# Hash bits of three heads: one test over 128 partitions and copies within SBUF, in place of four tests of six partitions

## The chip, the core and the metric

The kernel runs on one core of a Trainium2 chip. A core has five engines that work side by side, each through its own queue of instructions in order: TensorE (PE, matrix products, with PEld for its weight loads), VectorE (DVE), ScalarE (ACT), GpSimd (POOL) and SyncE (SP, which issues transfers). SBUF is the working memory of 128 partitions, PSUM the smaller one into which TensorE writes; GpSimd does not read PSUM here. The metric is the time of one execution on the device in microseconds (us). All times below that are not durations count from the start of the profiled span.

## The reference

Attention within hash buckets, and then a feed-forward layer with a maximum of three products. Shapes: batch 4, 8 heads, 768 positions, head width 64, 6 hash bits; the second part has 3072 tokens, width 512, inner width 768.

```python
q_bits = (np.einsum('bhsd,dk->bhsk', q, proj) > 0)     # k_bits in the same way
q_bucket = np.sum(q_bits * powers, axis=-1)
mask = q_bucket[:, :, :, None] == k_bucket[:, :, None, :]
scores = np.where(mask, scale * q @ k.T, -1e9)
attn = softmax(scores) @ v
h = np.maximum(np.maximum(x @ w1, x @ w2), x @ w3)     # x: attn with the heads side by side
out = h @ w_out
```

## The kernel before

**The mask as part of the product.** A tile S holds, for one head, the 64 rows of the transposed q (or k) in partitions 0 to 63 and the hash bits, as +0.5 or -0.5, in the partitions from 64 on. One product of 70 rows then gives the score plus the number of bits that agree, and the exponential of ScalarE (L292) subtracts the full number, so that pairs of other buckets come out at nearly zero. So before the scores of a head can be computed, its q and k must be transposed and scaled (the "placement") and its bits tested and put under them.

**Batch 0 in pairs of heads.** The first batch comes in four pairs of heads. For each pair, side (1 is k, 0 is q) and head, the steps are: three transposes by TensorE into a PSUM tile mp (pair_turn, L132); a copy of mp into an SBUF tile T32 by VectorE or ScalarE (pair_keep, L138); a scaled copy into S by GpSimd (pair_place, L143); the hash product of T32 with the projection (TensorE, into a PSUM tile bp); and the test of the hash against zero, which gives the bits. The positions of a head are held in two halves ("par" 0 and 1 of 384 each), one in partitions 0 to 63 of T32 and one in 64 to 127.

For pair 0 and pair 1 the hash is made head by head: first_hash (L171) multiplies with two six-column pieces of the projection, so that for side and par the six bits lie in partitions 32j to 32j+5 of bp, j = 2 side + par. first_bits (L177) tests one such piece: VectorE reads six partitions of bp from PSUM and writes 6x384 bits to their place in S. A head takes four of these. For pairs 2 and 3, pair_hash (L149) fills 128 partitions, tests them in one operation into a tile "bits", and four transfers by SP carry them into S.

**The order of the work** is written out by hand. The scores are cut into units u = 0, 1, 2, ... of two key blocks each: scores(u) issues two products (L290) into an sc tile and one exponential. Twelve units cover a pair in batch 0: units 0 to 5 are head 0 of pair 0, 6 to 11 head 1, 12 to 23 pair 1. `when(u, f)` hangs other work on unit u, in the order of its registration. For pair 1 the transposes and copies stand on units 1, 1, 2 and 4, the hashes (head_hash) on 3 and 6, the bits (head_bits) on the same units and the ones after. The tuple `cs` says for each of the four copies, in the order key and query of head 0, key and query of head 1, whether ScalarE (1) or VectorE (0) makes it. The copies of pair 2 stand on units 5, 6, 9 and 10; the second is the key copy of head 1.

Two rings of PSUM tiles matter. Up to unit 10, mp and bp tiles take the tags m0 to m3 in turn, so that a tile waits until the one four places earlier has been read. From unit 11 on there is a third sc buffer, laid over two of these tags, so unit 11 waits until the tiles in them have been read, and mp and bp share the two that are left.

**Projection tiles.** pst is the projection as loaded. GpSimd copies it into pj2 (L470, 128x32, the two halves of the projection interleaved for the two pars) and into pj (L472, for the later batches' quads of heads), before its first placement.

The call of the bits in the first head's second half and in pair 1:

```python
for side, par in ((1, 0), (0, 0), (1, 1)):
    first_bits(bp, side, 1, par)          # pair 0, head 1; the fourth on unit 1
...
def head_bits(pi, hd, n):
    side, par = ((1, 0), (0, 0), (1, 1), (0, 1))[n]
    first_bits(parts[pi, hd], side, hd, par, pi)
```

Of the kernel before, what the change touches and what calls it, by code (L numbers as in the profile page):

```python
# [9 lines left out]
FP32 = mybir.dt.float32  # L10
FP16 = mybir.dt.float16
BF16 = mybir.dt.bfloat16
AluOp = mybir.AluOpType
# [4 lines left out]
def kernel(  # L18
# [12 lines left out]
    nc = tc.nc  # L31
    B, H, S, D = q.shape
    NBITS = proj.shape[1]
    P = 128
    NM = S // P
    HALF = S // 2
# [5 lines left out]
    Q = 32  # L42
# [15 lines left out]
    konst = ctx.enter_context(tc.tile_pool(name="konst", bufs=1))  # L58
# [1 line left out]
    t32_pool = ctx.enter_context(tc.tile_pool(name="t32", bufs=3))  # L60
    t16_pool = ctx.enter_context(tc.tile_pool(name="t16", bufs=2))
    s_pool = ctx.enter_context(tc.tile_pool(name="spool", bufs=6))
    b_pool = ctx.enter_context(tc.tile_pool(name="bpool", bufs=2))
    vo_pool = ctx.enter_context(tc.tile_pool(name="vopool", bufs=4))
    small = ctx.enter_context(tc.tile_pool(name="small", bufs=4))
    ys_pool = ctx.enter_context(tc.tile_pool(name="yspool", bufs=1))
# [11 lines left out]
    def lay_out(**tags):  # L78
        rings.update(tags)
        if "pool" in rings:  # L80
            third.close()
        rings["pool"] = third.enter_context(tc.tile_pool(name="third_ps", bufs=1, space=bass.MemoryType.PSUM))
# [3 lines left out]
    def ps_tile(name, kind="ms"):  # L86
        if kind == "ms" and spare:
            return spare.pop(0)
        tag = rings[kind].pop(0)
        rings[kind].append(tag)  # L90
        shape = [P, 2, 512] if kind == "sc" else [P, 512]
        return (rings["pool"] if tag in ("s2", "m2", "m3") else fixed_ps).tile(shape, FP32, tag=tag, name=name)
# [2 lines left out]
    iden = konst.tile([P, P], FP32, name="iden")  # L95
    pj = konst.tile([P, 2, Q], FP32, name="pj")
    pj2 = konst.tile([P, Q], FP32, name="pj2")
    pst = konst.tile([Q, 2, NBITS], FP32, name="pst")
    ones = konst.tile([P, 3, Q], FP16, name="ones")
    warm = konst.tile([P, HALF], FP16, name="warm")  # L100
# [7 lines left out]
    nat, t32, t16, s_of, where, v_at = {}, {}, {}, {}, {}, {}  # L108
# [6 lines left out]
    def s_tile(name):  # L115
        if name not in s_of:
            s_of[name] = s_pool.tile([D + KB, 4, S], BF16, tag="S", name="S")
        return s_of[name]


    def load_pair(pi, eng, sides=(1, 0), h0=0, h1=2):
        if pi not in nat:
            start_set(pi, [(0, 2 * pi), (0, 2 * pi + 1), (1, 2 * pi), (1, 2 * pi + 1)])
        n = nat[pi].rearrange("p (s h w) -> p s h w", s=2, h=2)
        for side in sides:
            src = (q, k)[side][0, 2 * pi + h0 : 2 * pi + h1].rearrange("h (p c) d -> p h (c d)", p=P)
            eng.dma_start(n[:, side, h0:h1, :], src)
# [12 lines left out]
    def pair_place(pi, side, par, h0=0, h1=2):  # L140
        o = s_tile(pi)[0:D, 2 * side + h0 : 2 * side + h1, par * HALF : (par + 1) * HALF]
        i_ = t32[pi][par * D : (par + 1) * D, side, h0 * HALF : h1 * HALF].rearrange("d (h n) -> d h n", n=HALF)
        nc.gpsimd.tensor_scalar(out=o, in0=i_, scalar1=RS, scalar2=1.0, op0=AluOp.mult, op1=AluOp.mult)  # L143
# [27 lines left out]
    def first_hash(bp, side, hd, pi=0):  # L171
        for par in range(2):
            j = 2 * side + par
            nc.tensor.matmul(bp[Q * j : Q * j + NBITS, 0:HALF], pj2[:, par : 2 * NBITS : 2],  # L174
                             t32[pi][:, side, hd * HALF : (hd + 1) * HALF], start=True, stop=True)

    def first_bits(bp, side, hd, par, pi=0):  # L177
        j = 2 * side + par
        nc.vector.tensor_scalar(out=s_of[pi][D : D + NBITS, 2 * side + hd, par * HALF : (par + 1) * HALF],  # L179
                                in0=bp[Q * j : Q * j + NBITS, 0:HALF], scalar1=0.0, scalar2=0.5,  # L180
                                op0=AluOp.is_gt, op1=AluOp.subtract)


    def load_quad(side, g, xs, eng):
# [263 lines left out]
    def when(u, f, *args):  # L448
        at.setdefault(u, []).append(lambda: f(*args))

    with tc.manual_schedule():
# [7 lines left out]
        load_pair(1, nc.sync)  # L459
        load_pair(2, nc.sync)  # L460
        nc.gpsimd.memset(pj[:], 0.0)
        nc.vector.memset(pj2[:], 0.0)
        nc.vector.memset(ones[:], 1.0)
        nc.vector.memset(ones[:, 1, Q // 2 :], 0.0)
        nc.vector.memset(ones[:, 2, : Q // 2], 0.0)
        for t in at_tiles:
            nc.vector.memset(t[:, :, HALF : HALF + 2], 1.0)
        for hd in range(2):
            for u in range(2):
                nc.gpsimd.tensor_copy(pj2[hd * D + u * Q : hd * D + (u + 1) * Q, hd : hd + 2 * NBITS - 1 : 2], pst[:, u, :])  # L470
        for x in range(4):
            nc.gpsimd.tensor_copy(pj[x * Q : (x + 1) * Q, :, x : x + 4 * NBITS - 3 : 4], pst[:])  # L472
        lay_out(sc=["s0", "s1"], ms=["m0", "m1", "m2", "m3"])
        wp = ps_tile("wp", "sc")[:, 0, :]
        mq, mk, bk, bq = ps_tile("mp"), ps_tile("mp"), ps_tile("bp"), ps_tile("bp")
# [4 lines left out]
        pair_keep(0, 1, 0, mk)  # L480
        pair_keep(0, 0, 0, mq, nc.scalar.copy)
        first_hash(bk, 1, 0)
        first_hash(bq, 0, 0)
        mk1 = ps_tile("mp")
        pair_turn(0, 1, 1, mk1)
        for side, par, mp, bp in ((1, 0, mk, bk), (0, 0, mq, bq), (1, 1, mk, bk)):
            first_place(side, 0, par, mp)
            first_bits(bp, side, 0, par)
        pair_place(0, 0, 1, 0, 1)
        pair_keep(0, 1, 1, mk1, nc.scalar.copy)  # L490
        first_bits(bq, 0, 0, 1)
        mq1 = ps_tile("mp")
        pair_turn(0, 0, 1, mq1)
        pair_keep(0, 0, 1, mq1, nc.scalar.copy)
        scores(0)
        rest = []

        def first_rest():
            bp = ps_tile("bp")
            rest.append(bp)  # L500
            for side in (1, 0):
                first_hash(bp, side, 1)
                for par in range(2):
                    pair_place(0, side, par, 1, 2)
            for side, par in ((1, 0), (0, 0), (1, 1)):
                first_bits(bp, side, 1, par)
            t32.pop(0)

        when(0, first_rest)
        when(1, lambda: first_bits(rest[0], 0, 1, 1))  # L510

        def head_hash(pi, hd, last):
            bp = parts[pi, hd] = ps_tile("bp")
# [4 lines left out]

        def head_bits(pi, hd, n):
            side, par = ((1, 0), (0, 0), (1, 1), (0, 1))[n]  # L520
            first_bits(parts[pi, hd], side, hd, par, pi)

        parts = {}
        for pi, us, hs, offs, by_head, cs in ((1, (1, 1, 2, 4), (3, 6), (0, 0, 1, 1), 0, (1, 1, 0, 1)),):
            for u, c, (side, hd) in zip(us, cs, ((1, 0), (0, 0), (1, 1), (0, 1))):
                when(u, pair_group, pi, side, hd, nc.scalar.copy if c else nc.vector.tensor_copy)
                if hd == 1 or by_head:
                    for par in range(2):
                        when(u, pair_place, pi, side, par, *((hd, hd + 1) if by_head else ()))
            for hd in range(2):  # L530
                when(hs[hd], head_hash, pi, hd, hd == 1)
                for n in range(4):
                    when(hs[hd] + offs[n], head_bits, pi, hd, n)
# [16 lines left out]
        for g in range(2, NPAIR // 2):  # L550
# [3 lines left out]
            for n, side in enumerate((1, 0)):  # L554
                name = (side, g)
# [122 lines left out]
```

## Time and profile before

| what | us |
|---|---|
| median of 3 runs (260.29 to 260.9) | 260.55 |
| profiled execution, its own time | 260.33 |
| its span, first to last instruction | 258.6 |
| TensorE busy | 252.3 |
| VectorE busy | 207.9 |
| ScalarE busy | 182.0 |
| GpSimd busy | 77.7 |
| L179 (bits of six partitions), 16 times | 8.9 |
| L138 on VectorE, 8 times | 4.5 |
| L143 (placements), 17 times | 12.4 |

The time of the profiled execution is 1.7 us more than the span of its instructions. The busy time of TensorE contains matmuls that overlap in its pipeline. Rows of a timeline give start, duration, engine (a q behind it: its queue), line, operation, tile written and tiles read, shapes, and how often; in brackets stands idle time of the engine before it and what ended it. Tile names lose their numbers: T is T32, pj stands for pj and pj2.

### The profile page before, as it was taken

Reading aid. Unit: us, or ns where it says so; the run is one execution under the profiler, and the core shown is the slowest. Engines: PE = TensorE matmul, PEld = TensorE weight load, DVE = VectorE, ACT = ScalarE, POOL = GpSimd, SP = SyncE. Lnnn points to the kernel's source line nnn. Section 1 sums busy time; section 2 is a strip of 40 time slices with the busy share of each in tenths; the row PEclk is TensorE's granted clock in tenths of the full one; section 3 lists DMA queues with packets and bytes.
Section 4 is the critical chain, followed back from the end, with each engine's and each line's share of the span. In section 5 each row is a group of like instructions: output and inputs, shape, how many; then the busy total and the mean of one; then the engine's idle time right before and its main releaser. Section 6 shows DMA issues by size and latency. Waiting matters only on the chain.

```text
span 258.6 us, 5894 instructions
## 1 busy us (share of the span) xinstructions
PE 252.3 (98%) x2207; PEld 139.0 (54%) x2207; DVE 207.9 (80%) x474; ACT 182.0 (70%) x276; POOL 77.7 (30%) x128
## 2 busy tenths in 40 slices
PE   7999999999999999999999999999999999999994
PEld 3454444555555555555555555555555555555552
DVE  2794989999989997999989998998758984884450
ACT  3999887939994589909995589909995689612322
POOL 3599921694617119221416116100000000000000
PEclk9999999999999999999999999999999999999998
DMA  7998997659983707670283806320120003001203
GB/s 213 379 243 123 188 267 194 190 135 204 168 252 83 178 3 163 202 193 11 57 248 68 193 3 135 109 71 11 42 81 3 0 3 122 3 0 38 87 0 122
DMA packets 22251, 30.92 MB, mean 120 GB/s; under 512 B 3056, under 2 KB 17744, under 8 KB 22224
## 3 DMA queue, kind: packets, MB, share of 16 engines
q0 software_dynamic: 9088, 12.59, 25.6%
q1 hardware_dynamic: 12848, 17.58, 21.2%
q8 instruction: 17, 0.28, 0.5%
q10 hardware_dynamic: 288, 0.39, 0.5%
q14 instruction: 10, 0.08, 0.1%
HBM read 25.17 MB, written 6.29 MB: 122 GB/s over the span
## 4 chain that ended last, share of the span: by engine, by line
PE 91%; DVE 6%; issue 1%; ACT 0%; DVEq 0%
PE l L405 36%; PE sc L290 23%; PE l L436 12%; PE av L317 10%; PE bp L218 3%; PE mp L132 2%; DVE xT L386 2%; DVE T L197 1%; PE bp L174 1%; PE sm L367 1%; PE wp L477 1%; DVE S L179 1%; PE bp L154 1%; DVE rb L374 1%; PE l L425 1%
## 5 line engine op out<-in xcount | busy, mean ns | idle before, releaser
L292 ACT ACTIVATE AT<-sc 128x768 f16<-128x768 f32 x192 | 152.6, 823 | 45.9 <-PE sc L290 39.2
L405 PE MATMUL l<-xT,w_sb 128*128 128x384 f16 x568 | 112.1, 325 | 0.0
L290 PE MATMUL sc<-S 72*128 72x384 bf16 (+1 forms) x384 | 91.7, 326 | 0.7 <-ACT AT L292 0.6
L405 PEld LDWEIGHTS <-w_sb 128*128 128x128 f16 x576 | 55.4, 97 | 39.2 <-DVE xT L386 1.2
L414 DVE TENSOR_TENSOR ht<-ht,l 128x384 f16<-128x384 f16 x95 | 52.2, 550 | 20.6 <-PE l L405 17.9
L290 PEld LDWEIGHTS <-S 72*128 72x128 bf16 (+1 forms) x384 | 36.1, 98 | 33.9 <-issue 8.3
L202 POOL TENSOR_SCALAR T<-T 128x768 bf16<-128x768 f32 x24 | 22.4, 934 | 79.1 <-DVE T L197 42.8
L436 PE MATMUL l<-wout_sb,ht 128*128 128x512 f16 x138 | 36.0, 378 | 0.0
L342 DVE TENSOR_TENSOR As<-As,AT 128x768 f16<-128x768 f16 x52 | 33.9, 653 | 2.1
L317 PE MATMUL av<-AT,vo 128*32 128x385 f16 x744 | 34.2, 327 | 0.2 <-DVE xT L386 0.2
L342 DVE TENSOR_TENSOR As<-AT,AT 128x768 f16<-128x768 f16 x52 | 29.6, 568 | 4.6 <-ACT AT L292 4.6
L412 ACT CAST ht<-l 128x384 f16<-128x384 f32 x47 | 22.5, 478 | 10.4 <-DVE ht L414 5.9
L317 PEld LDWEIGHTS <-vo 128*32 128x32 f16 x768 | 19.5, 96 | 15.3 <-issue 6.4
L197 DVE STREAM_TRANSPOSE T<-nat 128x384 f32<-128x384 f32 x48 | 26.5, 564 | 0.2 <-DMA S<-bits 0.2
L386 DVE SCALAR_TENSOR_TENSOR xT<-av,sv,rb 128x384 f16<-128x384 f32 (+1 forms) x35 | 21.6, 618 | 1.2
L436 PEld LDWEIGHTS <-ht 128*128 128x128 f16 x138 | 13.3, 97 | 12.5
L344 DVE TENSOR_TENSOR As<-As 128x384 f16<-128x384 f16 x48 | 17.2, 358 | 1.7
L440 ACT COPY osb<-l 128x512 f32<-128x512 f32 x23 | 13.4, 582 | 6.5 <-PE l L436 6.5
L248 POOL DMA_DIRECT2D vo<-in_v_dram x24 | 13.3, 570 | 2.8 <-DMA wout_sb<-in_moe_w_out_dram 1.6
L143 POOL TENSOR_SCALAR S<-T 64x768 bf16<-64x768 f32 (+1 forms) x17 | 12.4, 731 | 3.7 <-DVE T L138 1.8
L179 DVE TENSOR_SCALAR S<-bp 6x384 bf16<-6x384 f32 x16 | 8.9, 554 | 2.4 <-PE bp L174 2.1
L374 DVE STREAM_TRANSPOSE rb<-rr 128x384 f32<-128x384 f32 x16 | 9.1, 566 | 0.1
(55 smaller groups left out, 115.8 us busy)
## 6 DMA issues: line engine op xcount, KB each, us to landing
out_dram<-osb SPq DMA_DIRECT2D x23, 256.0 KB
S<-T SPq DMA_DIRECT2D x48, 96.0 KB
nat<-in_k_dram POOLq DMA_DIRECT2D x16, 192.0 KB, 4.7
nat<-in_q_dram POOLq DMA_DIRECT2D x16, 192.0 KB, 5.7
w_sb<-in_moe_w_dram POOLq DMA_DIRECT2D x12, 192.0 KB, 4.6
vo<-in_v_dram POOLq DMA_DIRECT2D x24, 96.0 KB, 5.3
nat<-in_k_dram SPq DMA_DIRECT2D x10, 192.0 KB
nat<-in_q_dram SPq DMA_DIRECT2D x8, 192.0 KB
```

The lines of the kernel that those rows point to most:

```text
L197: nc.vector.transpose(t32[name][:, u, half * HALF : (half + 1) * HALF], i_)
L202: nc.gpsimd.tensor_scalar(out=t16[name][:, u, :], in0=t32[name][:, u, :], scalar1=RS, scalar2=1.0, op0=AluOp.mult, op1=AluOp.mult)
L290: nc.tensor.matmul(sc[:, j, 0:HALF], s_of[kn][0 : D + nb, kx, m * P : (m + 1) * P], s_of[qn][0 : D + nb, qx, qh * HALF : (qh + 1) * HALF], ...
L292: nc.scalar.activation(at_tiles[u % NAT][:, :, 0:HALF], sc[:, :, 0:HALF], ActFn.Exp, bias=-SCALE * 0.25 * nb, scale=SCALE)
L317: nc.tensor.matmul(av[r * Q : (r + 1) * Q, 0 : HALF + 1], vt[:, x, c + w : c + D : D // Q], at_of(g, m, hd)[:, 0 : HALF + 1], start=(m == ...
L342: nc.vector.tensor_tensor(out=t[:], in0=old, in1=new, op=AluOp.add)
L344: nc.vector.tensor_tensor(out=t[:, 0, :], in0=t[:, 0, :], in1=t[:, 1, :], op=AluOp.add)
L386: nc.vector.scalar_tensor_tensor(out=o, in0=av[p0:p1, 0:HALF], scalar=sv[p0:p1, :], in1=rc[p0:p1, :], op0=AluOp.add, op1=AluOp.mult)
L405: nc.tensor.matmul(ps[:, 0:HALF], w_sb[wi][:, jc, fb * P : (fb + 1) * P], xt[:, jc, :], start=(jc == 0), stop=(jc == NJC - 1))
L412: nc.scalar.copy(as_l(hts[fb]), l)
L414: nc.vector.tensor_tensor(out=as_l(hts[fb]), in0=as_l(hts[fb]), in1=l, op=AluOp.max)
L436: nc.tensor.matmul(ps[:, 0:DM], hts[fb][:, tb * P : (tb + 1) * P], wout_sb[:, fb, :], start=(fb == 0), stop=(fb == NFB - 1))
```

## The change

- A projection tile pj1 (128x2x32) is added: for par 0 and 1 it has the six columns, and zeros up to 32. VectorE clears it, and GpSimd fills it with four copies where it filled pj2 before. pj2 is now filled from pj1 with two copies, and pj with four from pst as before, all on unit 2, ahead of that unit's placements.
- first_hash multiplies with 32 columns in place of six, so that all 128 partitions of bp are written.
- For head 1 of pair 0 and both heads of pair 1 the four tests become one test over 128 partitions from PSUM into an SBUF tile "bits" (head_hashed), and four copies by VectorE of 6x384 within SBUF to their places in S (bits_place), at the places in the order where the tests stood. Head 0 of pair 0 stays with first_bits. The pool of bits tiles has three buffers in place of two.
- The copies of pair 1's two query tiles go from ScalarE to VectorE.

```diff
-    b_pool = ctx.enter_context(tc.tile_pool(name="bpool", bufs=2))
+    b_pool = ctx.enter_context(tc.tile_pool(name="bpool", bufs=3))
...
-            nc.tensor.matmul(bp[Q * j : Q * j + NBITS, 0:HALF], pj2[:, par : 2 * NBITS : 2],
+            nc.tensor.matmul(bp[Q * j : Q * (j + 1), 0:HALF], pj1[:, par, :],
...
+    def head_hashed(bp, hd, pi):
+        t = hashed[pi, hd] = b_pool.tile([P, HALF], BF16, tag="bits", name="bits")
+        nc.vector.tensor_scalar(out=t[:], in0=bp[:, 0:HALF], scalar1=0.0, scalar2=0.5,
+                                op0=AluOp.is_gt, op1=AluOp.subtract)
+
+    def bits_place(side, hd, par, pi):
+        j = 2 * side + par
+        nc.vector.tensor_copy(s_of[pi][D : D + NBITS, 2 * side + hd, par * HALF : (par + 1) * HALF],
+                              hashed[pi, hd][Q * j : Q * j + NBITS, :])
...
+        nc.vector.memset(pj1[:], 0.0)
...
-        for hd in range(2):
+        for par in range(2):
             for u in range(2):
-                nc.gpsimd.tensor_copy(pj2[hd * D + u * Q : hd * D + (u + 1) * Q, hd : hd + 2 * NBITS - 1 : 2], pst[:, u, :])
-        for x in range(4):
-            nc.gpsimd.tensor_copy(pj[x * Q : (x + 1) * Q, :, x : x + 4 * NBITS - 3 : 4], pst[:])
+                nc.gpsimd.tensor_copy(pj1[par * D + u * Q : par * D + (u + 1) * Q, par, 0:NBITS], pst[:, u, :])
+
+        def more_projections():
+            for hd in range(2):
+                nc.gpsimd.tensor_copy(pj2[hd * D : (hd + 1) * D, hd : hd + 2 * NBITS - 1 : 2], pj1[hd * D : (hd + 1) * D, hd, 0:NBITS])
+            for x in range(4):
+                nc.gpsimd.tensor_copy(pj[x * Q : (x + 1) * Q, :, x : x + 4 * NBITS - 3 : 4], pst[:])
+
+        when(2, more_projections)
...
+            head_hashed(bp, 1, 0)
             for side, par in ((1, 0), (0, 0), (1, 1)):
-                first_bits(bp, side, 1, par)
+                bits_place(side, 1, par, 0)
...
-        when(1, lambda: first_bits(rest[0], 0, 1, 1))
+        when(1, bits_place, 0, 1, 1, 0)
...
-            first_bits(parts[pi, hd], side, hd, par, pi)
+            if n == 0:
+                head_hashed(parts[pi, hd], hd, pi)
+            bits_place(side, hd, par, pi)
...
-        for pi, us, hs, offs, by_head, cs in ((1, (1, 1, 2, 4), (3, 6), (0, 0, 1, 1), 0, (1, 1, 0, 1)),):
+        for pi, us, hs, offs, by_head, cs in ((1, (1, 1, 2, 4), (3, 6), (0, 0, 1, 1), 0, (1, 0, 0, 0)),):
```

## The prediction

> **What bounds the kernel now.** I read the page's first sections, then the chain of waits from 9 to 18 us, then the timelines of VectorE, ScalarE and GpSimd over the first 30 us, and last the rows of single operations that resemble the new ones.
>
> The page says where the span is spent:
>
> ```profile
> PE 252.3 (98%) x2207; PEld 139.0 (54%) x2207; DVE 207.9 (80%) x474; ACT 182.0 (70%) x276; POOL 77.7 (30%) x128
> ...
> ACT  3999887939994589909995589909995689612322
> POOL 3599921694617119221416116100000000000000
> ```
>
> TensorE is the bound as a whole, and from 45 us on its rows follow one another with hardly a hole. So a delay or a gain made before then goes to the end at its full size. The edits all lie in the first 20 us, where ScalarE and VectorE are nearly full. The chain of waits there:
>
> ```profile
> 11.17 0.56 DVE S L179
> 11.73 0.14 issue
> 11.87 0.83 PE bp L174 x8
> ...
> 15.76 0.34 PE sc L290 x2
> 16.10 0.02 issue
> 16.12 0.82 ACT AT L292
> ```
>
> The fourth bits operation of head 1 ends at 11.72 and frees a PSUM buffer that the next hash (pair 1, head 0) needs. That hash delays the scores behind it, and so on to the scores of unit 8, for which ScalarE waits until 16.12. From there ScalarE runs without a hole to 26.16 (an exponential starts every 0.70 us, a copy takes 0.36), and then TensorE is full. So the question is when units 8 to 12 reach ScalarE. The same stretch on three engines (timelines; start, duration):
>
> ```profile
> 9.46 2.26 DVE L179 TENSOR_SCALAR S<-bp 6x384 bf16<-6x384 f32 x4 [0.64 <-PE bp L174]
> 11.75 0.56 DVE L138 COPY T<-mp 128x384 f32<-128x384 f32 x1
> 12.76 2.26 DVE L179 TENSOR_SCALAR S<-bp 6x384 bf16<-6x384 f32 x4 [0.45 <-PE bp L174]
> ...
> 16.77 0.56 DVE L138 COPY T<-mp 128x384 f32<-128x384 f32 x1
> ```
> ```profile
> 10.57 0.86 ACT L138 COPY T<-mp 128x384 f32<-128x384 f32 x2
> ```
> ```profile
> 9.89 0.94 POOL L244 DMA_DIRECT2D vo<-in_v_dram  x1
> 12.49 1.73 POOL L143 TENSOR_SCALAR S<-T 64x768 bf16<-64x768 f32 x2 [1.66 <-DVE T L138]
> 14.43 1.73 POOL L143 TENSOR_SCALAR S<-T 64x768 bf16<-64x768 f32 x2 [0.21 <-ACT T L138]
> ```
>
> ScalarE's two copies are pair 1's key and query of head 0; a third, the query of head 1, stands at 13.87 (0.47). VectorE is busy throughout, and GpSimd works beside it. Today that does no harm: L179 and L138 read PSUM, and their durations (549 to 562 ns) are the same with and without a GpSimd operation beside them.
>
> **What a VectorE operation from SBUF to SBUF meets.** Two rows of later stages:
>
> ```profile
> 55.33 0.41 DVE L327 TENSOR_SCALAR rr<-ys 128x12 f32<-128x12 f32 x1
> 34.50 0.17 DVE L327 TENSOR_SCALAR rr<-ys 128x12 f32<-128x12 f32 x1
> 54.98 1.53 POOL L254 DMA_DIRECT2D wout_sb<-in_moe_w_out_dram  x2
> 71.90 1.20 DVE L342 TENSOR_TENSOR As<-AT,AT 128x768 f16<-128x768 f16 x1 [0.20 <-ACT AT L292]
> 71.86 0.82 POOL L202 TENSOR_SCALAR T<-T 128x768 bf16<-128x768 f32 x1 [1.13 <-issue]
> ```
>
> L327 reads one SBUF tile and takes 0.17 alone, 0.41 at 55.33, ending when GpSimd's first L254 issue ends (55.74); at 27.18 it ended within 0.03 of the end of an L143 placement. L342 takes 0.52 alone and 1.20 here, ending 0.41 after GpSimd's operation: it was held until that was over. The ten new copies that run before 18 us are operations of this kind, put among placements of 0.82 us.
>
> **The parts, one by one.**
>
> Up to 9.46 us nothing on the path moves. The memset of pj1 (twice L462's 0.085) lies in VectorE's 3.20 us of idle time before 4.92; its cover is that idle time. GpSimd's four copies into pj1 stand where those into pj2 stood (4 x 0.18). The four copies into pj (5.48 to 6.41, 0.93) leave, so the first placement may come 0.75 earlier; its reader, the scores of unit 3, run at 10.3, so it gains nothing. They return, with two for pj2, behind the v load at 10.83: six copies of 0.18 to 0.20 with 0.05 between them, 1.45 us, in GpSimd's idle 1.66 before 12.49. They end at 12.3, and no placement waits; without that cover the placements would slip, and their reader, unit 12, runs only at 18.0. pj2 is first read at 20.3. No DMA is added or passes another on SP's or GpSimd's queue. The hash matmuls write 32 rows in place of 6, with the same 384 columns; the 32-row hash of L154 takes 0.498 where L174's takes 0.486, with weight loads of 0.108 and 0.086 beside it, 0.05 per head at most. The third bits buffer costs nothing.
>
> Bits: three heads had 4 x 0.554 with gaps, 2.26 us each. They now have one operation over 128 partitions (0.56, as L158's 128x384 from PSUM) and four copies of 6x384. The copy's price is not in the trace: below, L327's 0.17 (12 elements, all fixed cost); above, L344's 0.36 (384 16-bit elements, SBUF to SBUF, but two inputs). A copy has one input of those 384, so I take the middle, 0.26, and 0.02 between copies. "VectorE: DVE Perf Modes" of the Trainium skill (The perf-mode tier table) has 693 ns for 2048 elements in its fastest mode; less 1664 elements at four per cycle (0.43) that makes an estimate of 0.26, and the sum would be the same. A copy at one element per cycle would cost 0.56: a rival.
>
> The PSUM buffer is now free at 10.02 instead of 11.72, so the wait at 11.87 goes. What is late next is pair 1's query copy, which moves from ScalarE (ended 11.43) to VectorE, behind the four copies of bits.
>
> Beside nothing else: copies 10.05 to 11.14, query copy 11.17 to 11.73, query hash at 11.85 instead of 12.20: 0.35 early. The second moved copy then ends at 14.11, before TensorE needs it (14.41), and unit 8 comes 0.35 early. With 0.17 per copy TensorE's own order is the limit (unit 4's scores end issuing at 11.31): 0.42 early. With 0.36 the hashes are 0.06 late, and the copy of pair 2 that frees unit 11's PSUM buffer ends at 17.92 instead of 17.33; unit 11's exponential has 0.33 to spare and is 0.3 late.
>
> With GpSimd holding them (a held copy ends 0.13 after GpSimd's operation, since held rows of L342 and L327 hid 0.11 to 0.15 of their own time): the first passes, the second is held by the v load to 10.96, the last two take turns with the 0.18 us copies: 11.58. Query copy to 12.16, query hash at 12.28: 0.08 late. The key copy ends at 12.75, GpSimd's placement runs 12.93 to 13.76. The next bits operation ends at 13.40, its first copy is held until 13.89. Now it matters who goes first:
> - GpSimd's second placement goes ahead (13.89 to 14.71): second copy 14.84, query copy 15.43, query hash 15.53 instead of 14.77: 0.76 late. The next two copies meet a placement (15.72 to 16.54; done 16.67), then pair 2's copy, the third bits operation to 17.84, two copies to 18.41, and pair 2's second copy ends at 19.0 instead of 17.33. Unit 11 is 1.65 late less its 0.33: **1.3**.
> - VectorE's second copy goes ahead: query copy 14.74, hash 0.08 late; two held pairs later pair 2's copy ends at 18.11, 0.78 late: **0.45**.
>
> Nothing shows which; I take the middle, 0.9. From unit 11 ScalarE and then TensorE carry it to the end. If each software DMA issue holds the copies as L254 did (10.05 to 10.83, 17.5 to 18.6), another 0.4 and 0.6 come on top: 2.3.
>
> "SBUF — State Buffer" of the Trainium skill (SBUF: two separate sides) speaks against this change: VectorE in its two-port modes and GpSimd share a port pair, which one holds for a whole instruction while the other is blocked. By that rule the held sum applies; the rows of L327 and L342 agree, while at 82.63 an L327 beside an L248 issue took its usual 0.18.
>
> The ScalarE side: two copies go (0.47 each, 0.36 of its time). ScalarE waits for TensorE at 13.17 (0.32) and 16.12 (0.35), so less work there only makes these waits longer. I cost it at nothing.
>
> **Sum.** The profiled execution took 260.33 (span 258.6 and 1.7 around it), 0.22 under the median 260.55. 260.33 + 0.9 = 261.2, or **261.45** against the median.
>
> **Rivals.**
> 1. The copies are not held. For it: six partitions are little, and the L327 at 82.63 passed. Against: the held rows above. 0.35 to 0.42 early: 260.15.
> 2. Faster: ScalarE is the bound from 8 us on, and losing two copies starts unit 8 by 2 x 0.36 = 0.72 earlier, 259.85. It decides if unit 8's scores are ready before 15.4. For it: ScalarE's slices of 9. Against: its two waits for scores.
> 3. The copies run at one element per cycle, 0.56 each as L179. Ten of them put pair 2's second copy at 19.8 instead of 17.33: 2.5 late, 2.2 at unit 11: 262.75. Against: L344 does twice that rate.
>
> **Chances.** What a measurement of this kernel can tell from no change is about 0.2%, 0.52 us. Held: 0.58, of it 0.08 at its light end, under 0.52. Not held: 0.22, within 0.52. ScalarE: 0.16. One element per cycle: 0.04. So faster 0.16, same 0.30, slower 0.54. The range runs from the unheld 260.1 to 262.85 (2.3 late); outside it are rival 2 and a little above.
>
> **What would show it.** Right: L179's successor has one 0.56 row per head; copies of 6x384 with a shortest near 0.26 and others of 0.5 to 0.9 that end just after a GpSimd row; pair 1's query copy on VectorE near 12; a later start of the exponential that stood at 18.21. Wrong: copies all equally short, and TensorE's hash at 11.85 or before. What would make the prediction wrong most easily is the order of turns at the port, or that a copy of six partitions doesn't need it.

## The result, and the profile after

The changed kernel takes 261.87 us (median of 5 runs, 261.43 to 262.38). The kernel before, timed beside it, takes 260.29 us (260.28 to 260.9). The ratio is 1.0048, with an interval from 1.0035 to 1.0062: the change makes the kernel 0.9 to 1.6 us slower. The prediction was 261.45 us, between 260.1 and 262.85. The profiled execution of the changed kernel took 262.38 us, the longest of the five, with a span of 260.6.

The page of the changed kernel, its sections of busy time and of slices (PE, and the slices of ScalarE and GpSimd):

```profile
PE 254.4 (98%) x2207; PEld 140.2 (54%) x2207; DVE 209.6 (80%) x480; ACT 181.4 (70%) x274; POOL 78.5 (30%) x130
...
ACT  3869896948996399918996499918996589612322
POOL 2679940666625218141325216000000000000000
```

TensorE is the bound as before. ScalarE's third slice (13.0 to 19.5 us) has fallen from 9 to 6: it waits there. The chain of waits of the changed kernel between 11 and 20 us (start, duration, what) shows for what:

```profile
11.76 0.33 PE sc L304 x2
12.08 1.29 PE bp L175 x8
...
13.40 0.57 DVE bits L189
...
13.99 0.25 DVE S L194
...
14.26 0.79 DVE S L194
...
15.08 0.56 DVE T L139
...
15.67 0.25 DVE S L194
...
15.94 0.79 DVE S L194
...
16.76 0.56 DVE T L139
17.32 0.47 DVE bits L189
...
17.81 0.31 DVE S L194
...
18.14 0.25 DVE S L194
...
18.42 0.57 DVE T L139
...
19.04 0.48 PE sc L304 x2
```

In the kernel before, the chain ran through TensorE from 11.87 on, with one exponential of ScalarE at 16.12. Now it runs through VectorE from 13.40 to 18.99, with 0.04 us at most between two operations. The line numbers are new: L189 is the test over 128 partitions, L194 the copy of bits, L139 the copy into T32, L144 the placement, L175 the hash, L304 the scores, L306 the exponential. In the first two pairs of bits copies shown, the first takes 0.25 and the second 0.79. GpSimd's timeline for the same time (start, duration, operation, how often) says why:

```profile
10.57 0.95 POOL L258 DMA_DIRECT2D vo<-in_v_dram  x1
11.57 0.43 POOL L489 COPY pj<-pj 64x6 f32<-64x6 f32 x2
12.06 0.97 POOL L491 COPY pj<-pst 32x12 f32<-32x12 f32 x4
13.12 1.82 POOL L144 TENSOR_SCALAR S<-T 64x768 bf16<-64x768 f32 x2
15.72 1.80 POOL L144 TENSOR_SCALAR S<-T 64x768 bf16<-64x768 f32 x2 [0.78 <-DVE T L139]
```

Cut to 14.1 to 14.9 us, the same timeline shows the second of these placements by itself:

```profile
14.02 0.92 POOL L144 TENSOR_SCALAR S<-T 64x768 bf16<-64x768 f32 x1
```

The placement ends at 14.94, and the copy that began at 14.26 ends at 15.05, 0.11 later. The one at 15.94 ends at 16.73 in the same way, 0.12 after the placement that ended at 16.61. All twelve copies together (count, shortest, median and longest in ns):

```profile
L194 DVE COPY S<-bits x12: 252/268/791, 10.7 to 19.3; 6x384 bf16<-6x384 bf16 x12
```

So ScalarE's exponentials wait for the scores. Its timeline, before and then after, has 0.74 and 1.34 us of idle time where the kernel before had 0.32 and 0.35:

```profile
13.17 0.81 ACT L292 ACTIVATE AT<-sc 128x768 f16<-128x768 f32 x1 [0.32 <-PE sc L290]
16.12 3.62 ACT L292 ACTIVATE AT<-sc 128x768 f16<-128x768 f32 x5 [0.35 <-PE sc L290]
```
```profile
13.82 2.22 ACT L306 ACTIVATE AT<-sc 128x768 f16<-128x768 f32 x3 [0.74 <-PE sc L304]
17.37 3.05 ACT L306 ACTIVATE AT<-sc 128x768 f16<-128x768 f32 x4 [1.34 <-PE sc L304]
```

**How the stages are compared.** Executions differ in when TensorE is granted its full clock. The trace's record of it begins 4.59 us after the start in the profile of before, 6.89 in that of after, and 3.83 to 6.80 in the others, with no order by kernel. The matmuls agree: the first six transposes of after start 0.21 us apart up to 5.05, those of before 0.11 apart from 4.61 on. The first exponential starts between 7.9 and 8.8 us accordingly. Below, the starts of the exponentials are therefore compared after the two kernels' units 2 have been laid on each other. That still leaves some 0.2 us of doubt, since VectorE's chain doesn't follow TensorE's clock: laid on unit 0 instead, the kernel of experiment 1 is 0.16 less late everywhere. By this count the changed kernel is 0.64 us late at unit 8, 0.79 at unit 11, 0.90 at unit 20, 1.10 at unit 29 and 1.33 at the last.

### The profile page after: what moved, and what is told of

It is laid out like the page before. It is cut to its first block, busy times and chain, and to the rows that moved or that the text cites. A ratio compares the mean times of both kernels' runs of the same rounds, so it can differ in the third digit from the quotient of the medians.

```text
span 260.6 us, 5898 instructions
## 1 busy us (share of the span) xinstructions
PE 254.4 (98%) x2207; PEld 140.2 (54%) x2207; DVE 209.6 (80%) x480; ACT 181.4 (70%) x274; POOL 78.5 (30%) x130
## 4 chain that ended last, share of the span: by engine, by line
PE 90%; DVE 8%; issue 0%
PE l L419 35%; PE sc L304 22%; PE l L450 11%; PE av L331 10%; PE bp L232 3%; PE mp L133 2%; DVE xT L400 2%; DVE T L211 1%; PE bp L175 1%; PE sm L381 1%; PE wp L498 1%; DVE S L194 1%; PE bp L155 1%; DVE T L139 1%; DVE rb L388 1%; PE l L439 1%
## 5 line engine op out<-in xcount | busy, mean ns | idle before, releaser
L306 ACT ACTIVATE AT<-sc 128x768 f16<-128x768 f32 x192 | 152.8, 820 | 47.8 <-PE sc L304 41.4
L304 PE MATMUL sc<-S 72*128 72x384 bf16 (+1 forms) x384 | 91.8, 326 | 1.1 <-ACT AT L306 0.6
L304 PEld LDWEIGHTS <-S 72*128 72x128 bf16 (+1 forms) x384 | 36.1, 98 | 34.3 <-issue 8.7
L331 PEld LDWEIGHTS <-vo 128*32 128x32 f16 x768 | 19.5, 96 | 15.4 <-issue 6.5
L144 POOL TENSOR_SCALAR S<-T 64x768 bf16<-64x768 f32 (+1 forms) x17 | 12.7, 745 | 5.1 <-ACT T L139 2.9
L139 DVE COPY T<-mp 128x384 f32<-128x384 f32 x10 | 5.5, 556 | 5.0 <-PE mp L133 4.9
```

The lines of the kernel that those rows point to most:

```text
L304: nc.tensor.matmul(sc[:, j, 0:HALF], s_of[kn][0 : D + nb, kx, m * P : (m + 1) * P], s_of[qn][0 : D + nb, qx, qh * HALF : (qh + 1) * HALF], ...
L306: nc.scalar.activation(at_tiles[u % NAT][:, :, 0:HALF], sc[:, :, 0:HALF], ActFn.Exp, bias=-SCALE * 0.25 * nb, scale=SCALE)
L331: nc.tensor.matmul(av[r * Q : (r + 1) * Q, 0 : HALF + 1], vt[:, x, c + w : c + D : D // Q], at_of(g, m, hd)[:, 0 : HALF + 1], start=(m == ...
```

## The experiments

The theory on record: GpSimd and VectorE take turns at a resource that the copies of bits need, each held copy lasts until 0.11 us after GpSimd's operation, and the delay reaches TensorE at unit 11. Its rivals here: the price of the edits themselves (the copies, or the wider hash, or the query copies that now stand in VectorE's queue), and a mere difference of how an execution begins. Each kernel was timed beside the kernel before, which took 260.57 us (experiments 1 to 4), 260.46 (5, 7, 8 and the first run of 6) and 260.55 (the second run of 6, and 9).

### 1. The same copies in another form

```diff
-        t = hashed[pi, hd] = b_pool.tile([P, HALF], BF16, tag="bits", name="bits")
-        nc.vector.tensor_scalar(out=t[:], in0=bp[:, 0:HALF], ...
+        t = hashed[pi, hd] = b_pool.tile([P, HALF + 6], BF16, ...)[:].rearrange("p (a c) -> p a c", a=3)
+        nc.vector.tensor_scalar(out=t[:, :, 0:P], in0=bp[:, 0:HALF].rearrange("p (a c) -> p a c", a=3), ...
...
-                              hashed[pi, hd][Q * j : Q * j + NBITS, :])
+                              hashed[pi, hd][Q * j : Q * j + NBITS, :, 0:P])
```

The bits lie in three blocks of 128 with a gap of two elements behind each. "VectorE: DVE Perf Modes" of the Trainium skill (What auto-detection actually checks) lets a copy use both ports only if the outermost dimensions of source and destination are both even or equal. Here the trace's record of a copy has 3 blocks of 128 as its source and one run of 384 as its destination. "SBUF — State Buffer" of the Trainium skill (Who interferes with whom) says that such a copy doesn't contend with GpSimd.

> The changed kernel, but the tile of bits is laid out as three blocks of 128 with a gap of two between them, so that a copy reads three blocks and writes one run of 384. The same 12 copies, the same order, GpSimd unchanged. By the condition in VectorE: DVE Perf Modes of the Trainium skill (What auto-detection actually checks) such a copy uses one port, since the outer counts (3 and 384) are neither both even nor equal. Theory 'held' (the copies wait for GpSimd's placements at the shared port): each copy takes about 0.36 us, all alike, none of 0.79, and the kernel is 0.3 us slower than before instead of 1.3 to 1.6. Rival 'price' (what costs the time is only that the copies and the two moved T copies fill VectorE): 12 copies longer by 0.1 each make it slower than the changed kernel, 2 us or more over before. Rival 'start' (the time is lost in the first 8 us): as the changed kernel.

260.98 us against 260.57; ratio 1.0018 (1.0009 to 1.0026). The twelve copies of this kernel:

```profile
L194 DVE COPY S<-bits x12: 344/344/348, 10.1 to 18.4; 6x384 bf16<-6x384 bf16 x12
```

None is held, though placements ran beside them as before (12.96 to 14.69 and 14.98 to 16.71). The price alone would have made this kernel slower than the changed one, since its copies cost 0.09 more each. It is faster by 0.78 us (0.30% of 260.6). As the cause of that loss the copies' own price is out, and so is the start of an execution. The two rules and the rows agree.

Yet 0.41 us are left that the holding doesn't explain. The prediction's sum for unheld copies of 0.36 had 0.3 late here, so the price of this form may be a part of it; for unheld copies of 0.26 it had 0.35 early. Experiment 4 comes back to this.

### 2 and 3. The placements of pair 1 left out

```diff
+        s_tile(0)
+        nc.vector.memset(s_tile(1)[0:D, :, :], 0.0)
...
-                if hd == 1 or by_head:
-                    for par in range(2):
-                        when(u, pair_place, pi, side, par, *((hd, hd + 1) if by_head else ()))
```

Both the changed kernel and the kernel before get this edit. It leaves out the scaled q and k of pair 1, whose rows are zero instead.

> The changed kernel, but GpSimd's four placements of pair 1 (0.82 us each) are left out, and the rows that they would fill are zeroed at the start, in VectorE's idle time; so the scores of pair 1 are not computed rightly. Held: the copies of pair 1 meet no placement and take 0.25 us, but for one or two beside the v load's issue and the projection copies; units 8 to 12 start 0.2 to 0.4 us earlier than in the kernel before, and the time is 0.1 to 0.4 us below the same cut made in the kernel before (next run). Price: the time stays 1.3 us or so above it, as GpSimd is not on the chain. Start: likewise.

> The same cut made in the kernel before: pair 1's four placements by GpSimd left out, its rows zeroed at the start. All theories: no change from the kernel before (within 0.2 us), since the bits of that kernel are read from PSUM and are never held, and unit 12 waits for no placement.

Before without placements: 260.63 against 260.57, ratio 1.0001 (0.9992 to 1.0011). So the placements cost the kernel before nothing. Its profile also shows how an early delay travels: its clock came 2.2 us later than in the profile of before, its first exponential 0.52 us later, and every exponential up to the last is 0.52 to 0.54 late.

The changed kernel without placements: 261.02, ratio 1.0015 (1.0006 to 1.0023). The expectation for it relative to the other was missed: 0.39 us slower, not 0.1 to 0.4 faster. Its copies, and GpSimd's only operation beside the eight of pair 1:

```profile
L194 DVE COPY S<-bits x12: 250/252/811, 10.4 to 18.1; 6x384 bf16<-6x384 bf16 x12
```
```profile
17.99 0.82 POOL L144 TENSOR_SCALAR S<-T 64x768 bf16<-64x768 f32 x1 [4.24 <-DVE T L139]
```

The 0.811 is the last copy, beside that placement of pair 2; one of 0.62 ended with the load of v. With the placements of pair 1, and the holding by them, 0.86 us of the loss are gone, and a rest of 0.4 remains as in experiment 1. That one copy of 0.62 stands ahead of the first query copy, so this kernel isn't free of holding either.

### 4. The tests back, the query copies left on VectorE

```diff
-            head_hashed(bp, 1, 0)
...
-                bits_place(side, 1, par, 0)
+                first_bits(bp, side, 1, par)
...
-            if n == 0:
-                head_hashed(parts[pi, hd], hd, pi)
-            bits_place(side, hd, par, pi)
+            first_bits(parts[pi, hd], side, hd, par, pi)
```

> The changed kernel with its 12 copies undone: each of the three heads again has four tests of six partitions from PSUM at the same places; pj1, the later pj2 and pj, and the two T copies on VectorE stay. Held: no SBUF-to-SBUF operation of VectorE is left in this stretch, so nothing is held; VectorE has 4 x 0.57 per head and two T copies more, which puts pair 2's second T copy 0.8 us later than before and the kernel 0.4 to 0.6 us over before, about 1 us under the changed kernel. Price: VectorE has 1.3 us more work than in the changed kernel (12 x 0.57 against 3 x 0.57 and 12 x 0.27), so it is slower than the changed kernel. Start: as the changed kernel.

262.01 us, ratio 1.0056 (1.0041 to 1.007): 1.44 us over before, where 0.4 to 0.6 were expected. No bits are copied within SBUF in this kernel, so nothing is held in the first 20 us. What it keeps of the change is the wider hash and the two query copies on VectorE. Its hash is the key to the rest of 0.4. The timeline of TensorE before, then after, then in this kernel; the row behind each hash is the next product of scores. The last row of the first two shows the hash in part: of before the matmuls that have begun by 12.0, of after the weight loads with what they waited for:

```profile
11.87 0.83 PE L174 MATMUL bp<-T,pj 128*6 128x384 f32 x8 [0.40 <-DVE S L179]
12.63 0.50 PE L290 MATMUL sc<-S 70*128 70x384 bf16 x2
...
11.87 0.51 PE L174 MATMUL bp<-T,pj 128*6 128x384 f32 x4 [0.40 <-DVE S L179]
```
```profile
12.01 1.34 PE L175 MATMUL bp<-T,pj 128*32 128x384 f32 x8
13.28 0.50 PE L304 MATMUL sc<-S 70*128 70x384 bf16 x2
...
12.01 0.14 PEld L175 LDWEIGHTS bp<-T,pj 128*32 128x32 f32 x4 [0.32 <-ACT T L139]
12.51 0.14 PEld L175 LDWEIGHTS bp<-T,pj 128*32 128x32 f32 x4 [0.35 <-DVE T L139]
```
```profile
12.49 1.34 PE L175 MATMUL bp<-T,pj 128*32 128x384 f32 x8 [0.40 <-ACT AT L306]
13.76 0.50 PE L304 MATMUL sc<-S 70*128 70x384 bf16 x2
```

A head's hash is eight passes of four products, of the key's and the query's two halves. In the kernel before all four products have their first pass between 11.87 and 11.89 and their second between 12.19 and 12.21, one beside the other, and the scores follow 0.76 after the start. In the changed kernel the key's two run at 12.01 and the query's only at 12.51, because the query copy ends at 12.46. The scores follow 1.27 after the start, but again 0.77 after the query's products. In this kernel the wait before the hash ends with the fourth test, at 12.35 (the row names ScalarE), the query copy stands behind the four tests and ends at 12.94, its products start at 12.99, and the scores follow 0.77 later. So in all three the scores go by the half of the hash whose copy comes last. What the key's half gains from the freed PSUM buffer is lost in the wait for the query's half.

By this the rest of 0.4 can be estimated. The prediction's 11.85 for the query's products of an unheld change is level with before's 11.88. In experiment 1 the four copies ahead of the query copy cost 4 x 0.09 more than unheld ones of 0.25, in experiment 2 the load of v lengthened one of them by 0.36. Either makes the query's products about 0.36 late, and unit 8 is 0.49 and 0.33 late there. No run has these copies at 0.25 with none of them held, so that this would be level with before isn't shown.

### 5. The query copies back on ScalarE, nothing else

```diff
-        for pi, us, hs, offs, by_head, cs in ((1, ..., 0, (1, 0, 0, 0)),):
+        for pi, us, hs, offs, by_head, cs in ((1, ..., 0, (1, 1, 0, 1)),):
```

> The changed kernel with the two query T copies of pair 1 back on ScalarE; the 12 copies of bits stay as they are. Theory 'held and late query' (the copies of bits are held by GpSimd's placements, and beside that the hash of pair 1, head 0, waits for its query copy because all four of its matmuls start together): the hash starts at 11.5 on the scale of the kernel before, unit 5 is 0.3 to 0.4 us early, and then the copies of the next two heads are held for 0.79 us as in the changed kernel and pair 2's second T copy comes about 1 us late; the time is 0.6 to 1.0 us over before, 0.4 to 0.8 under the changed kernel. Rival 'held alone' (where the T copies are made makes no difference): as the changed kernel, 1.3 to 1.6 over before. Rival 'ScalarE' (ScalarE's load sets the pace): slower than the changed kernel by 0.7.

Five executions took 262.04 to 264.66 us, with a median of 263.19, which is 2.7 us over before; a sixth took 268.26 (with it the median is 263.46). The ratio is 1.0112 (1.0082 to 1.0143). That it is slower than before was expected, the size not, and against the changed kernel it is slower where 0.4 to 0.8 faster was expected. Units 5 to 10 come 0.36 us earlier than before, from unit 2 on, which fits the freed PSUM buffer. But GpSimd's four placements now run in one row, and with them three copies of 0.89 us. VectorE and GpSimd in this kernel:

```profile
12.92 3.09 DVE L194 COPY S<-bits 6x384 bf16<-6x384 bf16 x4
```
```profile
12.36 3.54 POOL L144 TENSOR_SCALAR S<-T 64x768 bf16<-64x768 f32 x4
```

TensorE then works for 0.63 of the 2.40 us before 18.40, with a last wait of 1.19 for pair 2's copy, and its granted clock falls to half. Time by stages of this kernel (stretch, length, busy time of PE with its count, PEclk behind POOL; other columns are not used here):

```profile
16.00:18.40 2.40, 0.63 (x4) 0.29 (x3) 2.26 (x7) 1.94 (x3) 1.10 (x3) 0.99 1.09 185
18.40:20.00 1.60, 1.60 (x7) 1.19 (x6) 1.19 (x3) 0.81 (x1) 1.52 (x2) 0.50 0.89 152
20.00:21.80 1.80, 1.80 (x9) 1.40 (x8) 0.24 (x1) 1.38 (x3) 1.35 (x4) 0.51 0.31 29
21.80:25.00 3.20, 3.20 (x25) 1.67 (x25) 1.36 (x3) 3.07 (x5) 2.56 (x4) 1.00 0.77 114
```

The delay grows from 0.93 at unit 11 to 1.69 at unit 13, whose exponential starts at 21.61, while the clock is at 0.5, and to 2.34 at unit 20. The times of the five go with the mean clock that they were granted, from 262.04 at 0.999 to 264.66 at 0.986, so 1.6 us over before are left in the one that lost almost no clock. No step of the prediction had this. "TensorE: Matmul & The Clock Gate" of the Trainium skill (Part 1: The HAM clock gate) has the clock at half until some 3.4 us of sustained work have passed; the trace has it at half for 3.41 us here.

### 6. Both: the other form, and the query copies on ScalarE

This kernel was run twice, the second time beside the first kernel of experiment 9.

> Both causes taken away: the copies of bits in the form that reads three blocks (one port, 0.344 us each in the first such run, none held), and the two query T copies back on ScalarE. Held and late query: unit 5 and all units behind it start 0.3 to 0.4 us earlier than before, and the kernel is 0.3 to 0.4 us faster than before. Held alone: 0.4 over before, as the first run with one port. ScalarE: 1 us over before.

> The kernel with the one-port copies and pair 1's query copies of batch 0's second pair on ScalarE, a second time, beside the next. Theory (held copies and the late query hash are the loss; without both the change gains what its shorter wait is worth): 0.2 to 0.5 us faster than before, copies 0.344 to 0.348, units 5 to 19 about 0.36 early. If the gain of the first time was only the spread between executions, this one is within 0.15 us of before or slower.

260.09 us against 260.46, ratio 0.9985 (0.9972 to 0.9997); the second time 260.48 against 260.55, ratio 0.9988 (0.9974 to 1.0003). The ratios agree within their intervals; the second by itself doesn't exclude no change. Both profiles have units 5 to 19 earlier than before by 0.36 to 0.38 from unit 2 on. The hash and the scores behind it in the chain of the first:

```profile
12.04 0.85 PE bp L175 x8
12.89 0.43 PE sc L304 x2
```

The hash starts without a wait and is as short as before. So with neither the holding nor the late query hash the idea does what its freed buffer promises, some 0.36 us in the profiles. Compared with experiment 1 (query copies on VectorE, behind copies of 0.344), 0.30% to 0.33%, some 0.8 us, came from the query copies alone.

### 7. The projection and the wider hash alone

```diff
-    b_pool = ctx.enter_context(tc.tile_pool(name="bpool", bufs=2))
+    b_pool = ctx.enter_context(tc.tile_pool(name="bpool", bufs=3))
...
-            nc.tensor.matmul(bp[Q * j : Q * j + NBITS, 0:HALF], pj2[:, par : 2 * NBITS : 2],
+            nc.tensor.matmul(bp[Q * j : Q * (j + 1), 0:HALF], pj1[:, par, :],
...
+        when(2, more_projections)
```

This kernel is before with pj1, the late copies into pj and pj2, the hash of 32 rows and the third buffer; the tests stay as they were.

> Of the changed kernel only pj1, the later pj2 and pj, the 32-column hash and the third bits buffer are kept; tests of six partitions and T copies as in the kernel before. Held and late query, and held alone: no change from before (within 0.2 us). Rival 'start' (something in the first 8 us or the wider hash costs time): 0.3 to 0.5 us slower than before.

260.44 us against 260.46, ratio 1.0001 (0.999 to 1.0012). These edits cost nothing.

### 8. The placements of pair 1 in halves

```diff
-                        when(u, pair_place, pi, side, par, *((hd, hd + 1) if by_head else ()))
+                        for h in range(2):
+                            when(u, pair_place, pi, side, par, h, h + 1)
```

A held copy lasts as long as what holds it; here GpSimd's operations are eight of 0.51 in place of four of 0.83.

> The changed kernel, but each of GpSimd's four placements of pair 1 is made in two, one per head (0.51 us each, as the placements of pair 0, against 0.82). GpSimd works longer in all, but holds the port for a shorter time at once. Held: the longest copies of pair 1's bits take about 0.48 us instead of 0.79, and the kernel is 0.3 to 0.7 us faster than the changed kernel, 0.7 to 1.1 over before. Rivals that do not know of the port (price, late query alone): as the changed kernel.

The longest copies beside pair 1's placements are 0.43 to 0.57 in place of 0.79, and unit 11 is 0.48 late in place of 0.79. That is the holding by turns, in its length. The time is 261.51 us against 260.46, ratio 1.0040 (1.0027 to 1.0052). That is within the 0.7 to 1.1 over before that was expected, but its interval overlaps with that of the changed kernel, so that it is faster than this one isn't shown. By the profile the end is 1.33 late as there: between units 42 and 54 this kernel lost another 0.55, and by what stays open.

### 9. The later losses: one small operation in the same form

The changed kernel's delay grows by another 0.2 at unit 29. There VectorE adds a constant to twelve sums (L341, rr from ys), which stood at 0.28 in the profile of before (L327 there). VectorE before, then VectorE and GpSimd after:

```profile
27.18 0.28 DVE L327 TENSOR_SCALAR rr<-ys 128x12 f32<-128x12 f32 x1
```
```profile
28.58 0.62 DVE L341 TENSOR_SCALAR rr<-ys 128x12 f32<-128x12 f32 x1
...
27.43 1.73 POOL L144 TENSOR_SCALAR S<-T 64x768 bf16<-64x768 f32 x2
```

It ends at 29.20, after a placement that ends at 29.16. Both profiles of experiment 6 have it at 0.62 as well. The edit writes it in three padded blocks, so that it takes the form that wasn't held:

```diff
-        nc.vector.tensor_scalar(out=rr, in0=ys[:, 0 : HALF : Q // n], ...)
-        nc.vector.reciprocal(rr, rr)
+        w = n * HALF // Q // 3
+        rp = rpad[:].rearrange("p (a c) -> p a c", a=3)[:, :, 0:w]
+        nc.vector.tensor_scalar(out=rp, in0=ys[:, 0 : HALF : Q // n].rearrange("p (a c) -> p a c", a=3), ...)
+        nc.vector.reciprocal(rr.rearrange("p (a c) -> p a c", a=3), rp)
```

It was put into the kernel of experiment 6, into before, and into the changed kernel.

> As the former, and the sum that is made ready for its reciprocal (L341 of after, rr from ys) is written into a tile of three padded blocks, so that it too has the form that was not held; the reciprocal reads that tile and writes rr. If the holds of L341 at 27 to 29 us and near 56 us (0.616 and 0.406 us in place of 0.174) take back 0.2 to 0.3 us of the gain, L341 is 0.17 to 0.20 at every instance and this kernel is 0.5 to 0.8 us faster than before and 0.1 to 0.4 faster than the former. If those later losses have another cause, L341 is as short but the time is within 0.1 us of the former. If this small operation (12 or 24 elements) is held in any form, L341 stays at 0.4 to 0.6 at the first instance.

> The kernel before with the sum rr written into the padded tile, nothing else. In before's profile this operation was held by 0.10 us at 27.18 and by 0.24 us at 55.33; the kernel with one-port copies gained 0.41 us at these two places in its profile (of 0.98 between the medians). If that is this operation's worth by itself: 0.2 to 0.5 us faster than before, L327 0.17 to 0.20 everywhere. If it only takes back what the changed order of the first 20 us had added: within 0.15 us of before.

> The changed kernel with the sum rr written into the padded tile, its bits copies left as they are. If the later pieces of its loss (0.2 us at unit 29, where this operation took 0.616, and 0.2 us at units 49 to 50) are this operation's holds: 0.9 to 1.2 us over before in place of 1.3 to 1.6, with the start up to unit 20 as in the changed kernel (0.8 to 0.9 late from the own start). If they come from elsewhere: as the changed kernel, 1.3 to 1.6 us over before, with the rows short all the same.

The operation in the kernel of experiment 6, and with the edit (ten times each):

```profile
L341 DVE TENSOR_SCALAR rr<-ys x10: 173/180/616, 27.2 to 228.0; 128x24 f32<-128x24 f32 x6, 128x12 f32<-128x12 f32 x4
```
```profile
L344 DVE TENSOR_SCALAR rpad<-ys x10: 173/194/197, 26.3 to 226.6; 128x24 f32<-128x24 f32 x6, 128x12 f32<-128x12 f32 x4
```

- With experiment 6: 259.50 us against 260.55, ratio 0.9956 (0.9939 to 0.9972), 0.98 under the kernel of experiment 6 timed beside it, more than the 0.1 to 0.4 that was expected. **This beats both kernels**, by 0.7 to 1.6 us against before. The profiles have 0.41 of the 0.98: 0.15 at unit 29, the rest up to unit 36. The remainder stays open: in this profile the full clock came at 3.87 us, in that of the other at 6.80.
- In before: 260.44 against 260.55, ratio 0.9998 (0.9989 to 1.0007). By itself the edit is worth nothing that can be measured; the profile has 0.1.
- In the changed kernel: 261.58 against 260.55, ratio 1.0039 (1.0026 to 1.0051), 1.03 over before where the first theory gave 0.9 to 1.2. At unit 20 it is later than the 0.8 to 0.9 of that theory, but the profile no longer loses behind it: 1.13 late there, 0.93 at the last. The changed kernel went from 0.90 to 1.33 on that way. The intervals of the two ratios overlap, so that the 0.4 rests on the profiles.

### By stage

Lateness against before in us, from unit 2 on, at the start of the exponential named (negative is earlier), and the difference of the medians. Experiments 3 and 7 and the kernel before with the edit of 9 stay within 0.1 of before at all of these units:

| kernel | unit 8 | 11 | 20 | 29 | last | medians |
|---|---|---|---|---|---|---|
| after | 0.64 | 0.79 | 0.90 | 1.10 | 1.33 | +1.58 (1.25 by the ratio) |
| 1: other form | 0.49 | 0.48 | 0.42 | 0.62 | 0.53 | +0.41 |
| 2: after, no placements | 0.33 | 0.33 | 0.25 | 0.30 | 0.35 | +0.45 |
| 4: tests back | 0.96 | 0.96 | 1.09 | 1.15 | 1.32 | +1.44 |
| 5: query copies on ScalarE | -0.36 | 0.93 | 2.34 | 2.34 | 2.23 | +2.73 (of five) |
| 6: 1 and 5 together | -0.36 | -0.36 | -0.46 | -0.32 | -0.25 | -0.37, again -0.07 |
| 8: halves | 0.45 | 0.48 | 0.59 | 0.76 | 1.33 | +1.05 |
| 9: with 6 | -0.36 | -0.36 | -0.47 | -0.47 | -0.78 | -1.05 |
| 9: in after | 0.88 | 1.02 | 1.13 | 1.19 | 0.93 | +1.03 |

## Why the prediction was right, and where not

- **The bound, and that a delay goes to the end: right.** Experiment 3 shows 0.52 us carried from the first exponential to the last without a change.
- **No cost of the projection and the wider hash: right** (experiment 7, -0.02 us).
- **The prices: right.** The test over 128 partitions takes 0.56 and the unheld copy 0.252, where 0.26 was taken between 0.17 and 0.36. The rival of 0.56 per copy falls (rival 3).
- **The holding: right in its mechanism, and near in its size at unit 11** (0.79, where 0.9 was taken). The held copies end 0.11 to 0.12 after the placement (0.13 taken). Of the two orders of turns it was the one in which GpSimd's second placement goes ahead of VectorE's second copy, for which the prediction had 1.3 and not 0.9. The end of that stretch, pair 2's second copy, was worked out at 19.0 and stands at 18.98; but this execution began 0.6 later than that of before, so 0.6 of the holding didn't come. Two of the first four copies ran in 0.25 beside the load of v and one was lengthened by 0.12, where some 0.4 were counted, and the first copy behind the second test slipped in ahead of the second placement in 0.25 where 0.49 were counted. So 0.9 came near by luck: it was the mean of two orders of which the worse one holds (1.3), and that one was worked out some 0.6 too high.
- **The step that failed: "query hash at 11.85 instead of 12.20: 0.35 early".** 12.20 was the time of the second passes. The query's first pass stood at 11.88, beside the key's, and for the second head it stood at 14.46 where the prediction took 14.77. So a query copy that lets its hash start at 11.85 gains nothing: the scores follow the query's half. The prediction did see that the query copy is what is late next, but it made that lateness 0.32 too small. In the held sum ("0.08 late") this was hidden, because the copies ahead of the query copy were held 0.3 less than counted. The move of the two query copies is worth 0.8 us by experiment 6 against 1, beside copies of 0.344.
- **Rival 1, "not held": wrong.** The copies were held. And its 260.15 rests on the step above: with 11.88 as the reference an unheld change would be about level with before, 260.5 as an estimate. No run shows it, since in experiment 1 the copies cost 0.09 more each and in 2 some were still held; both were 0.4 over before.
- **Rival 2, ScalarE as the bound: wrong.** Unit 8's scores were to be ready before 15.4; they came at 17.3, which is 16.7 on the scale of before. Giving the two query copies back to ScalarE made experiment 6 faster than experiment 1.
- **The end: too low by 0.42 us.** As a change from before, 0.9 was taken and 1.25 came by the ratio (1.58 between the medians). "From unit 11 ScalarE and then TensorE carry it to the end" left out that GpSimd goes on holding VectorE's operations: L341 took 0.62 in place of 0.28 at unit 29. Behind unit 20 another 0.43 came on top by the profile, and with that operation in the other form it didn't (experiment 9; the intervals of the two times overlap). For the piece of 0.2 between units 48 and 54 no single row was found.

## What to carry to other kernels

Before an operation is moved from PSUM to within SBUF on VectorE, look what GpSimd does at that moment: a 0.25 us copy cost 0.79 beside a 0.82 us placement, while a form of the same copy that takes 0.344 alone was never held. Where a result needs several products that ran side by side, as the hash here, it comes with the product whose operand is ready last, and in a merged row the start to compare with is that of its first pass. And a wait that is removed is worth measuring without what was put in its place: the freed PSUM buffer was worth 0.36 us here, and two other edits of the same change took about twice that each (0.78 by experiment 1, 0.8 by 6 against 1).

## What was not expected of the hardware

- TensorE's full clock was granted between 3.83 and 6.89 us after the start, different from execution to execution of nearly the same first microseconds. The first exponential starts up to 0.9 us later with it, and the whole execution (0.53 to the end in experiment 3).
- One stretch in which TensorE worked for 0.63 of 2.40 us was followed by 3.4 us at half its clock (experiment 5), during which the delay grew from 0.93 to 1.69, and to 2.34 behind it.
- Three copies of six partitions in a row took 0.89 us each beside four placements in a row (3.54 for the four): GpSimd's next operation stood ahead of VectorE's next each time, so a copy of 0.25 moved at the pace of a placement.
